# Gated linear attention and an MLP on one core: more turning by DMA, and a new order

## The chip, the cores and the metric

The kernel runs on one core of a Trainium2 chip. The metric is the device time of one execution in microseconds. The engines are named as in the profile: PE (TensorE, matrix products; PEld is its weight load), DVE (VectorE), ACT (ScalarE), POOL (GpSimd) and SP (SyncE, which here issues every DMA).

## The reference

Four batches, eight heads, 768 steps, head size 48, all float32. The attention keeps a 48x48 state for each head, decays it by a gate and adds an outer product at each step. Its outputs, the heads side by side, are the 3072 rows of 384 that go through an MLP with a silu.

```python
f = 1.0 / (1.0 + np.exp(-f_logit))
for t in range(S):
    state = f[:, :, t, :, None] * state + np.einsum('bhd,bhe->bhde', k[:, :, t], v[:, :, t])
    y[:, :, t] = np.einsum('bhd,bhde->bhe', q[:, :, t], state)
x = y.transpose(0, 2, 1, 3).reshape(B * S, H * D)      # 3072 x 384
h = x @ w_in                                           # w_in 384 x 2048
out = (h / (1.0 + np.exp(-h))) @ w_out                 # w_out 2048 x 384
```

## The kernel before

The steps are cut into chunks of 128. A *unit* is one chunk of one batch with all eight heads; there are 24. Two units make a pair P (units 2P and 2P+1), and q, k, v, f_logit are mostly loaded by pairs. In the first eight units two chunks of each batch alternate; from unit 8 on a pair is one chunk of two batches. Pairs 0 to 2 keep their rows in another interleaving (`HALF = 3`), which is why they have tasks of their own below.

The whole kernel is a list of named tasks, the string `PLAN`, in the order in which they are emitted. A word is `kind_arguments/engine/slots`: `mo_9_2/PE` is task `mo` of unit 9, part 2, on PE. Each engine works its own tasks strictly in the order of the list and waits where an operand is not ready. A slot number says which of a class's buffers a result takes (`SLOTS`); class `ps` is the eight PSUM banks, `qk` has five buffers, `qkT` three, `yb` three, `xT` four. So the list sets the order on each engine and on the DMA queue, and which buffer must be free first.

The tasks of a unit, in the order of the data:

- `f`, `q`, `k`, `v` (line 253): loads, on SP. `wi`, `wo` (291, 295) load the weights, and `wic`, `woc` (300) cast them to bf16.
- `E`, `L` (260, 262, 264): exp and log on ACT, which give the log of the gate. `cs` (356, 360), or `csh` for pairs 0 to 2 (331 to 335): its running sum, by a triangular product on PE.
- `ia`, `a`, `al` (363, 365, 368): exponentials of that sum on ACT. `qg`, `ki` (238): q and k times these, into buffer `qk`, on DVE or POOL. `vb` (231, 233, 235): v cast to bf16.
- q and k are then turned, so that the head dimension lies on the partitions. Units 0 to 9 do it by `tq` (379): eight PE transpositions into one PSUM bank, then copies out of it by `qc`, `kc` (pairs 0 to 2, line 389) or `qkc` (units 6 to 9, line 381). Units 10 to 23 do it by `qkD` (391), a DMA transposition from buffer to buffer. `dT`, `kn` (395, 397) turn k back for units 0 to 5.
- `sc2` (276): the scores of both units of a pair, 16 products. `at` (400): times the triangle, on DVE. `y` (406, 410): outputs from the old state and the scores. `d`, `sd`, `su` (432, 437, 439, 444): the new state.
- `yc`: y to bf16 in buffer `yb`. `yT` (418): y turned by three PE transpositions, and `xc` copies it to `xT`. A task `yD` (426), which turns it by DMA, is in the code, but the list does not use it.
- `mi`, `si` (319, 316): first product of a pair in eight parts of six matmuls, and the silu on ACT; `mi1`, `si1` (309, 306) the same by single units for units 0 to 5, in four parts of twelve.
- `mo` (347): second product of a unit, in four parts of four matmuls of 384 columns, all into one bank. `oc` copies it out, `so` (353) stores it.
- `idle` (287): products with zeros, which fill PE's waits at the start.

Copies share the helper's lines 231 (ACT), 233 (DVE) and 235 (POOL). ACT holds one table of functions at a time; where the list changes between exp or log and silu, a table load is emitted (line 483).

Of the kernel before, what the change touches and what calls it, by code (L numbers as in the profile page):

```python
# [30 lines left out]
f_0_1/SP/0 f_2_3/SP/1 k_0_1/SP/0 q_0_1/SP/0 q_2_3/SP/1 k_2_3/SP/1 wi_2/SP/0 v_0/SP/0 v_1/SP v_2/SP/1 wi_4/SP/1 wi_0/SP/0 wi_1/SP/1 v_3/SP E_0_1/ACT  # L31
L_0_1/ACT/0 idle_0_10_512/PE/0 csh_0/PE/0,1 E_2_3/ACT L_2_3/ACT/1 ia_1/ACT/0 a_1/ACT/0 ia_0/ACT/1 a_0/ACT/1 ki_1/DVE/0 qg_1/DVE ki_0/DVE/1 qg_0/DVE
idle_1_3_512/PE/2 csh_1/PE/2,3 idle_2_5_256/PE/1 tq_1/PE/4 idle_3_4_256/PE/1 tq_0/PE/5 a_2/ACT/2 ia_3/ACT/2 a_3/ACT/0 kc_1/DVE/0 qc_0/DVE qg_2/DVE/2
qg_3/DVE/3 qc_1/ACT kc_0/ACT ia_2/ACT/0 al_2/ACT/0 al_0/ACT/1 ki_2/DVE ki_3/POOL idle_4_4_512/PE/1 dT_0/PE/6 dT_1/PE/7 sc2_0/PE/1,3,4,5 tq_2/PE/2
idle_5_4_256/PE/0 tq_3/PE/0 kn_1/DVE/0 kc_2/ACT/1 qc_2/ACT kc_3/ACT wic_2_1/POOL vb_0/POOL/0 wic_2_0/POOL wic_2_2/POOL vb_1/POOL/1 at_0_1/DVE/0
at_1_0/DVE/1 qc_3/DVE kn_0/DVE/1 at_0_0/DVE idle_6_4_512/PE/3 d_0/PE/7 dT_2/PE/3 sc2_1/PE/4,2,6,0 y_0/PE/1 vb_2/POOL/2 yc_0/ACT/0 kn_2/ACT/1
at_1_1/DVE sd_0/DVE/0 at_2_1/DVE/2 at_2_0/DVE idle_7_3_512/PE/5 yT_0/PE/5 dT_3/PE/7 d_1/PE/1 d_2/PE/2 y_2/PE/3 xc_0/DVE/0 sd_2/DVE/1 wic_4_1/DVE
wic_4_2/DVE kn_3/ACT/0 yc_2/ACT/1 wic_4_0/ACT su_0/POOL/0 wi_3/SP/2 wo_0/SP/3 wo_1/SP/4 f_4_5/SP/2 wo_2/SP/0 wo_3/SP/1 q_4_5/SP/2 k_4_5/SP/2 f_7/SP/3
v_4/SP/2 v_5/SP f_6/SP v_6/SP/3 f_8_9/SP/0 k_6/SP/3 q_7/SP/3 q_6/SP k_7/SP y_1/PE/4 mi1_0_1/PE/5 yT_2/PE/7 xc_2/ACT/1 wic_0_0/POOL wic_0_1/ACT
yc_1/DVE/2 sd_1/DVE/0 su_2/DVE/0 wic_1_0/DVE wic_1_1/DVE at_3_1/DVE/3 at_3_0/DVE vb_3/POOL/3 mi1_0_3/PE/2 yT_1/PE/3 mi1_2_1/PE/4 mi1_2_3/PE/7  # L40
mi1_2_0/PE/1 mi1_0_0/PE/0 y_3/PE/6 si1_2_3/ACT/0 si1_0_3/ACT/1 si1_2_0/ACT si1_0_0/ACT yc_3/ACT/0 wic_3_1/ACT si1_2_1/ACT si1_0_1/ACT xc_1/DVE
wic_3_0/POOL wic_3_2/DVE mi1_1_0/PE/7 mi1_1_1/PE/2 yT_3/PE/3 mi1_1_3/PE/1 mi1_2_2/PE/0 mi1_1_2/PE/6 mi1_0_2/PE/4 d_3/PE/5 sd_3/DVE/1 woc_2_1/DVE
woc_2_0/DVE woc_2_2/DVE su_3/DVE/0 woc_3_1/DVE su_1/DVE/0 woc_3_2/DVE woc_3_0/DVE woc_0_2/POOL woc_0_1/POOL woc_1_0/POOL woc_1_2/POOL woc_1_1/POOL
si1_1_0/ACT woc_0_0/ACT si1_2_2/ACT si1_1_3/ACT si1_1_1/ACT si1_0_2/ACT xc_3/ACT si1_1_2/ACT E_4_5/ACT L_4_5/ACT/2 mo_0_0/PE/7 mo_1_0/PE/0 mo_2_0/PE/1
mi1_3_0/PE/5 mo_1_1/PE mi1_3_1/PE/2 mi1_3_3/PE/4 mo_0_1/PE csh_2/PE/3,6 al_4/ACT/2 ia_4/ACT/1 a_5/ACT/1 a_4/ACT/2 ia_5/ACT/0 vb_5/POOL/4 vb_4/POOL/5
qg_5/DVE/4 qg_4/DVE/0 ki_4/DVE si1_3_1/ACT ki_5/DVE mo_1_2/PE mo_0_2/PE mo_2_1/PE mi1_3_2/PE/3 mo_0_3/PE mo_1_3/PE tq_4/PE/6 tq_5/PE/2 oc_1/DVE/0
qc_4/DVE/2 si1_3_0/ACT si1_3_3/ACT si1_3_2/ACT kc_4/ACT kc_5/DVE qc_5/DVE E_7/ACT oc_0/DVE/1 mo_3_0/PE/5 mo_3_1/PE dT_4/PE/4 sc2_2/PE/0,3,6,2
kn_4/DVE/1 at_4_0/DVE/0 at_4_1/DVE L_7/ACT/0 E_6/ACT mo_2_2/PE d_4/PE/7 mo_3_2/PE cs_7/PE/4 y_4/PE/0 sd_4/DVE/1 at_5_0/DVE/2 at_5_1/DVE L_6/ACT
yc_4/ACT/1 ia_7/ACT/2 al_7/ACT/3 su_4/POOL/0 dT_5/PE/3 mo_3_3/PE cs_6/PE/7 yT_4/PE/6 mo_2_3/PE y_5/PE/0 ia_6/ACT/1 E_8_9/ACT a_7/ACT/0 kn_5/DVE/0
xc_4/DVE/2 oc_3/DVE/2 a_6/ACT/1 L_8_9/ACT/1 al_6/ACT/4 vb_6/POOL/0 qg_7/POOL/1 ki_6/DVE/2 yc_5/DVE/2 qg_6/DVE oc_2/DVE/3 ki_7/DVE mi1_4_0/PE/2  # L50
mi1_4_1/PE/3 d_6/PE/6 mi1_4_3/PE/5 yT_5/PE/4 mi1_4_2/PE/0 tq_6/PE/7 tq_7/PE/1 f_10_11/SP/1 q_8_9/SP/0 v_7/SP f_12_13/SP/2 q_10_11/SP/1 k_8_9/SP/0
so_1/SP k_10_11/SP/1 v_8_9/SP/0 si1_4_0/ACT/2 qkc_6/ACT/0 si1_4_2/ACT si1_4_1/ACT si1_4_3/ACT xc_5/DVE qkc_7/DVE vb_7/POOL/2 sd_6/DVE/0 su_6/DVE/0
mi1_5_1/PE/4 mi1_5_0/PE/2 mi1_5_2/PE/7 mi1_5_3/PE/1 sc2_3/PE/0,6,3,5 si1_5_2/ACT si1_5_3/ACT si1_5_0/ACT si1_5_1/ACT at_7_1/DVE/1 at_6_1/DVE/3
at_7_0/DVE at_6_0/DVE mo_4_0/PE/7 mo_4_1/PE cs_8/PE/1 cs_9/PE/2 d_5/PE/5 d_7/PE/4 mo_5_0/PE/6 y_7/PE/3 y_6/PE/0 mo_4_2/PE mo_5_1/PE yc_6/DVE/0
sd_5/DVE/1 yc_7/DVE/1 sd_7/DVE/0 E_10_11/ACT L_10_11/ACT/2 ia_8/ACT/0 cs_11/PE/0 yT_6/PE/5 mo_5_2/PE yT_7/PE/3 mo_5_3/PE mo_4_3/PE cs_10/PE/4
E_12_13/ACT ia_11/ACT/1 al_8/ACT/5 a_9/ACT/2 a_11/ACT/0 L_12_13/ACT/0 ia_9/ACT/2 a_8/ACT/1 xc_6/DVE/3 xc_7/DVE qg_9/DVE/3 ki_8/DVE/0 su_7/DVE/0
qg_8/DVE al_11/ACT/6 ia_10/ACT/0 a_10/ACT/2 oc_4/ACT/4 al_9/ACT/7 al_10/ACT/0 ki_9/DVE oc_5/DVE/0 mi_3_1/PE/5 mi_3_7/PE/3 tq_8/PE/1 mi_3_0/PE/0
mi_3_2/PE/7 tq_9/PE/2 mi_3_3/PE/4 mi_3_6/PE/6 qg_11/POOL/4 qkc_8/DVE/1 qkc_9/DVE ki_10/DVE/2 vb_9/POOL/1 qg_10/POOL vb_8/POOL/3 ki_11/POOL
si_3_2/ACT/1 si_3_1/ACT si_3_7/ACT si_3_0/ACT si_3_3/ACT so_0/SP so_5/SP v_10_11/SP/1 v_12_13/SP/2 qkD_10/SP/2 qkD_11/SP k_12_13/SP/2 so_3/SP
q_12_13/SP/2 d_9/PE/1 mi_3_4/PE/7 sc2_4/PE/2,5,3,0 mi_3_5/PE/4 sd_9/DVE/0 at_8_0/DVE/0 at_8_1/DVE at_9_1/DVE/2 at_9_0/DVE si_3_4/ACT si_3_5/ACT  # L60
si_3_6/ACT vb_11/DVE/5 cs_12/PE/1 d_8/PE/7 mo_7_0/PE/2 cs_13/PE/5 mo_7_1/PE y_8/PE/4 mo_7_2/PE y_9/PE/6 yc_8/DVE/2 yc_9/DVE/0 su_5/POOL/0 a_12/ACT/1
al_12/ACT/1 sd_8/DVE/1 a_13/ACT/0 al_13/ACT/4 vb_10/ACT/4 ia_13/ACT/2 ia_12/ACT/0 mo_7_3/PE mo_6_0/PE/0 yT_9/PE/3 mo_6_1/PE yT_8/PE/4 mo_6_2/PE
sc2_5/PE/6,5,7,1 mo_6_3/PE at_10_1/DVE/1 at_10_0/DVE at_11_1/DVE/3 at_11_0/DVE xc_8/ACT/0 xc_9/ACT oc_7/ACT/1 ki_12/POOL/1 vb_13/POOL/2 ki_13/POOL/3
qg_12/DVE oc_6/DVE/0 vb_12/DVE/0 qg_13/DVE mi_4_1/PE/4 mi_4_5/PE/3 mi_4_7/PE/2 mi_4_0/PE/5 y_10/PE/6 y_11/PE/1 mi_4_3/PE/7 mi_4_2/PE/0 si_4_5/ACT/0
yc_10/ACT/1 si_4_7/ACT yc_11/DVE/0 yT_11/PE/3 yT_10/PE/6 mi_4_6/PE/2 mi_4_4/PE/1 xc_11/ACT/1 si_4_3/ACT si_4_0/ACT si_4_2/ACT si_4_1/ACT si_4_4/ACT
si_4_6/ACT xc_10/DVE su_9/DVE/0 su_8/POOL/0 mi_5_4/PE/6 mi_5_5/PE/3 mi_5_3/PE/7 mi_5_2/PE/5 mi_5_0/PE/0 mi_5_7/PE/4 mi_5_1/PE/1 mi_5_6/PE/2
q_14_15/SP/3 f_16_17/SP/3 qkD_13/SP/0 qkD_12/SP f_18_19/SP/0 f_14_15/SP/1 q_16_17/SP/0 k_14_15/SP/3 v_14_15/SP/3 so_7/SP k_16_17/SP/0 f_20_21/SP/2
si_5_4/ACT/2 si_5_5/ACT si_5_2/ACT si_5_0/ACT si_5_7/ACT si_5_1/ACT si_5_3/ACT si_5_6/ACT sc2_6/PE/6,3,5,0 mo_9_0/PE/4 d_11/PE/1 at_12_0/DVE/0
at_12_1/DVE at_13_0/DVE/2 at_13_1/DVE sd_11/DVE/1 mo_8_0/PE/7 mo_9_1/PE y_12/PE/2 d_10/PE/6 d_13/PE/3 mo_9_2/PE d_12/PE/5 mo_8_1/PE mo_8_2/PE
y_13/PE/0 su_11/POOL/0 yc_12/DVE/2 sd_10/DVE/0 sd_13/DVE/1 yc_13/DVE/0 E_14_15/ACT L_14_15/ACT/1 E_16_17/ACT L_16_17/ACT/2 cs_17/PE/1 mo_8_3/PE  # L70
cs_15/PE/2 yT_13/PE/6 yT_12/PE/3 mo_9_3/PE cs_14/PE/0 al_15/ACT/3 a_15/ACT/2 ia_15/ACT/1 al_17/ACT/2 a_17/ACT/1 ia_14/ACT/0 al_14/ACT/5 a_14/ACT/0
ia_17/ACT/2 xc_13/DVE/2 xc_12/DVE oc_8/DVE/2 su_10/POOL/0 qg_14/DVE/0 oc_9/DVE/1 ki_14/DVE sd_12/DVE/0 ki_15/POOL/4 ki_17/POOL/2 qg_15/POOL
mi_6_5/PE/6 mi_6_1/PE/3 mi_6_6/PE/2 mi_6_4/PE/7 mi_6_3/PE/0 mi_6_0/PE/1 mi_6_2/PE/4 mi_6_7/PE/5 so_8/SP v_16_17/SP/0 qkD_15/SP/1 qkD_14/SP
q_18_19/SP/1 so_9/SP si_6_6/ACT/1 si_6_1/ACT si_6_0/ACT si_6_5/ACT si_6_2/ACT si_6_4/ACT si_6_3/ACT si_6_7/ACT mo_10_0/PE/2 cs_16/PE/3 mo_11_0/PE/1
# [86 lines left out]
def kernel(  # L161
# [117 lines left out]
    def emit(kind, a, eng):  # L279
# [95 lines left out]
        elif kind == "tq":  # L375
            t_ps = bank16("tq", u).rearrange("p (j n c) -> p j n c", j=2, c=C)
            for j in range(2):
                for p in range(NP):
                    nc.tensor.transpose(t_ps[:, j, p, :], at("qk", u)[:, j, 2 * p:2 * p + 2, :], ident)  # L379
# [135 lines left out]
```

## Time and profile before

| | |
|---|---|
| median of 3 runs | 182.08 us (182.04 to 182.3) |
| profiled execution | 181.97 us, span 180.2 us |
| PE busy | 172.5 us, 96% of the span |
| ACT, DVE, POOL busy | 131.8, 103.7, 41.5 us |
| granted PE clock | 1.0 throughout |
| DMA | 33.86 MB, mean 188 GB/s |

The span is the time from the first to the last instruction that the profile shows; the execution's own time is 1.8 us longer. Lines are those of the kernel's source; a line can be a helper's, and is then told apart by the tiles that it writes and reads (`qkT<-qk` writes `qkT` from `qk`). "Idle before" is the time that an engine stood still ahead of an instruction, with what it waited for. The chain of work that ended last goes back from the last instruction to what released it, step by step.

### The profile page before, as it was taken

The numbers are of one execution on the slowest core, as the hardware profiler recorded it, in microseconds if no ns is written. First come the engines' busy times: TensorE is split into PE (matmuls) and PEld (weight loads), VectorE is DVE, ScalarE is ACT, GpSimd is POOL, SyncE is SP. The second block draws the span as 40 slices with busy tenths as digits, with TensorE's granted clock in tenths as the row PEclk, the third lists the DMA queues.
The fourth block names the chain that finished last, engine by engine and source line by source line (L and its number), as shares of the span: only waits on it lengthen the run. The fifth ranks groups of instructions, "written<-read, shape, count | busy, mean of one in ns | idle before, by whom it ended". The sixth has DMA issues, their size and how long they took to land.

```text
span 180.2 us, 4796 instructions
## 1 busy us (share of the span) xinstructions
PE 172.5 (96%) x1969; PEld 134.8 (75%) x1971; DVE 103.7 (58%) x217; ACT 131.8 (73%) x249; POOL 41.5 (23%) x67
## 2 busy tenths in 40 slices
...
GB/s 159 322 323 303 356 392 397 230 214 213 177 176 242 101 64 188 222 234 154 234 194 222 167 195 227 261 181 92 178 262 161 160 247 4 0 87 4 0 44 131
DMA packets 110933, 33.86 MB, mean 188 GB/s; under 512 B 105280, under 2 KB 109120, under 8 KB 110912
## 3 DMA queue, kind: packets, MB, share of 16 engines
...
## 4 chain that ended last, share of the span: by engine, by line
PE 88%; DMA 4%; ACT 3%; DVE 2%; issue 0%; ACTq 0%
PE ps L347 34%; PE ps L319 25%; PE ps L309 9%; PE ps L276 4%; PE ps L410 3%; PE ps L418 2%; PE ps L379 2%; PE ps L432 2%; PE ps L406 2%; DMA f<-in_f_logit_dram 2%; DMA qkT<-qk 2%; ACT qkT L231 2%; PE ps L356 2%; DVE qk L238 1%; PE ps L287 1%; PE ps L395 1%
## 5 line engine op out<-in xcount | busy, mean ns | idle before, releaser
L347 PE MATMUL ps<-w_out,hT 128*128 128x384 bf16 x384 | 70.5, 326 | 0.0
L319 PE MATMUL ps<-xT,w_in 128*128 128x256 bf16 x432 | 50.4, 273 | 0.0
L347 PEld LDWEIGHTS <-hT 128*128 128x128 bf16 x384 | 34.8, 98 | 19.4
L319 PEld LDWEIGHTS <-w_in 128*128 128x128 bf16 x432 | 45.1, 110 | 1.8
L316 ACT ACTIVATE hT<-ps 128x512 bf16<-128x512 f32 x72 | 37.3, 612 | 7.6 <-PE ps L319 7.4
L400 DVE TENSOR_TENSOR at<-ps,triu 128x512 bf16<-128x512 f32 x36 | 22.4, 684 | 18.3 <-PE ps L276 16.9
L233 DVE COPY ob<-ps 128x384 f32<-128x384 f32 x16 | 8.8, 550 | 19.5 <-PE ps L347 19.5
L483 ACT ACT_TABLE_LOAD x15 | 19.2, 1283 | 0.3
L309 PE MATMUL ps<-xT,w_in 128*128 128x128 bf16 x288 | 18.1, 219 | 0.0
L309 PEld LDWEIGHTS <-w_in 128*128 128x128 bf16 x288 | 16.8, 110 | 0.4
L238 POOL TENSOR_TENSOR st<-sd,al 48x192 bf16<-48x192 f32 x18 | 9.8, 547 | 29.3 <-DVE sd L437 11.5
L238 POOL TENSOR_TENSOR qk<-k,ia 128x384 bf16<-128x384 f32 x9 | 9.3, 1036 | 26.2 <-DMA k<-in_k_dram 9.6
L437 DVE TENSOR_TENSOR sd<-ps,st 128x384 f32<-128x384 f32 x16 | 8.8, 550 | 10.7 <-ACT hT L316 5.2
L238 POOL TENSOR_TENSOR qk<-q,av 128x384 bf16<-128x384 f32 x7 | 8.0, 1155 | 29.5 <-ACT av L365 29.5
L238 DVE TENSOR_TENSOR qk<-k,ia 128x384 bf16<-128x384 f32 x15 | 12.3, 836 | 4.0 <-ACT ia L363 4.0
L306 ACT ACTIVATE hT<-ps 128x512 bf16<-128x512 f32 x24 | 13.0, 628 | 0.1
L238 DVE TENSOR_TENSOR qk<-q,av 128x384 bf16<-128x384 f32 x17 | 10.5, 629 | 4.2 <-ACT av L365 3.8
L231 ACT COPY xT<-ps 128x384 bf16<-128x384 bf16 x10 | 5.0, 515 | 10.6 <-PE ps L418 10.6
L363 ACT ACTIVATE ia<-ps 128x384 f32<-128x384 f32 x24 | 11.7, 496 | 1.2 <-PE ps L356 0.7
L260 ACT ACTIVATE f<-f 128x768 f32<-128x768 f32 (+1 forms) x13 | 10.3, 792 | 2.2 <-DMA f<-in_f_logit_dram 2.1
L365 ACT ACTIVATE av<-ps 128x384 f32<-128x384 f32 x24 | 11.4, 501 | 0.0
L287 PE MATMUL ps<-zero 128*128 128x512 bf16 (+1 forms) x35 | 9.8, 411 | 1.3 <-DVE zero L461 1.2
...
## 6 DMA issues: line engine op xcount, KB each, us to landing
...
```

Of the source, the lines that this page charges most:

```text
L238: (nc.vector if eng == "DVE" else nc.gpsimd).tensor_mul(*a)
L260: nc.scalar.activation(e, e, AF.Exp, scale=-1.0)
L287: nc.tensor.matmul(at("idle", u)[:, 0:w], zero[:, 0:128], zero[:, 0:w], start=True, stop=True)
L306: return nc.scalar.activation(at("hT", u // 2)[:, 4 * m:4 * m + 4, i * C:(i + 1) * C], h, AF.Silu)
L309: nc.tensor.matmul(h[:, n, :], w_in_tile(4 * m + n, kk), at("xT", u // 2)[:, kk, i * C:(i + 1) * C], start=(kk == 0), stop=(kk == KT - 1))
L316: return nc.scalar.activation(at("hT", P)[:, 2 * j:2 * j + 2, :], h, AF.Silu)
L319: nc.tensor.matmul(h[:, i, :], w_in_tile(2 * j + i, kk), at("xT", P)[:, kk, :], start=(kk == 0), stop=(kk == KT - 1))
L347: nc.tensor.matmul(o, at("hT", P)[:, n, i * C:(i + 1) * C], w_out_sb[n // 4][:, n % 4, :], start=(n == 0), stop=(n == NT - 1))
L363: nc.scalar.activation(at("ia", u).rearrange("p h d -> p (h d)"), at("cs", u)[:, 0:HD], AF.Exp)
L365: nc.scalar.activation(at("av", u).rearrange("p h d -> p (h d)"), at("cs", u)[:, 0:HD], AF.Exp, scale=-1.0)
L400: nc.vector.tensor_mul(at("at", u)[:, r], at(f"s{r}", u).rearrange("p (n c) -> p n c", c=C), (triup if two else triu)[:, None, :].to_broad ...
L483: nc.scalar.preload_act_table_set(turn[n])
```

## The change

1. `qkD` is also used for units 6 to 9, in the place of `tq` and `qkc`: 18 in place of 14.
2. `yD` is used for units 12 to 21, in the place of `yT` and `xc`: ten.
3. In units 0 to 5 (`APART`) the turned k goes to a second PSUM bank (`tqk`), so that `qc` and `kc` read different banks.
4. The second product of units 22 and 23 goes by `moh`, `och`, `soh`: each column half of 192 in a bank of its own, copied and stored by itself.
5. The list is in a new order throughout, with new slots, and some tasks have another engine. `ki` and `qg` on POOL go from 16 to 24, table loads from 15 to 19, products with zeros from 37 to 29. `SLOTS` is as before.

```diff
+APART = {0, 1, 2, 3, 4, 5}
...
-"tq": lambda: [(("tq", u), "ps")],
+"tq": lambda: [((x, u), "ps") for x in (("tq", "tqk") if u in APART else ("tq",))],
+"moh": lambda: [(("oB" if a[1] else "o", u), "ps")], "och": lambda: [(("ob", u), "ob")],
...
+        elif kind == "moh":
+            w = d_model // 2
+            o = at("oB" if a[1] else "o", u)[:, 0:w]
+            for n in range(4 * a[2], 4 * a[2] + 4):
+                nc.tensor.matmul(o, at("hT", P)[:, n, i * C:(i + 1) * C], w_out_sb[n // 4][:, n % 4, a[1] * w:(a[1] + 1) * w],
+                                 start=(n == 0), stop=(n == NT - 1))
+        elif kind == "och":
+            w = d_model // 2
+            copy(eng, at("ob", u)[:, a[1] * w:(a[1] + 1) * w], at("oB" if a[1] else "o", u)[:, 0:w])
+        elif kind == "soh":
+            r0, w = b * S + c * C, d_model // 2
+            nc.sync.dma_start(out=out[r0:r0 + C, a[1] * w:(a[1] + 1) * w], in_=at("ob", u)[:, a[1] * w:(a[1] + 1) * w])
...
-            t_ps = bank16("tq", u).rearrange("p (j n c) -> p j n c", j=2, c=C)
             for j in range(2):
                 for p in range(NP):
+                    t_ps = bank16("tqk" if j and u in APART else "tq", u).rearrange("p (j n c) -> p j n c", j=2, c=C)
                     nc.tensor.transpose(t_ps[:, j, p, :], at("qk", u)[:, j, 2 * p:2 * p + 2, :], ident)
...
-            copy(eng, dst, bank16("tq", u)[:, 512 * j:512 * (j + 1)].rearrange("p (w c) -> p w c", c=64))
+            copy(eng, dst, bank16("tqk" if j and u in APART else "tq", u)[:, 512 * j:512 * (j + 1)].rearrange("p (w c) -> p w c", c=64))
```

The new list, in the places that the prediction speaks of. The start:

```
f_0_1/SP/0 f_2_3/SP/1 q_0_1/SP/0 k_0_1/SP/0 E_0_1/ACT f_4_5/SP/2 L_0_1/ACT/0 E_2_3/ACT idle_0_11_512/PE/0 csh_0/PE/0,1 v_0/SP/0 a_0/ACT/0 v_1/SP
ia_0/ACT/0 qg_0/DVE/0 a_1/ACT/1 ki_0/DVE q_2_3/SP/1 ia_1/ACT/1 qg_1/DVE/1 L_2_3/ACT/1 idle_1_8_512/PE/2 tq_0/PE/2,3 k_2_3/SP/1 ki_1/DVE E_4_5/ACT
kc_0/DVE/0 idle_2_4_256/PE/1 tq_1/PE/4,5 csh_1/PE/6,7 qc_0/DVE wi_3/SP/0 kc_1/ACT qc_1/DVE vb_1/POOL/0 al_0/ACT/0 vb_0/DVE/1 a_2/ACT/2
sc2_0/PE/1,3,2,4 wi_2/SP/1 L_4_5/ACT/2 dT_0/PE/5 qg_2/POOL/2 at_0_1/DVE/0 a_3/ACT/0 at_1_0/DVE/1 kn_0/ACT/0 idle_3_2_512/PE/0 csh_2/PE/0,3 qg_3/POOL/3
at_1_1/DVE al_2/ACT/1 ia_3/ACT/2 wi_1/SP/0 d_0/PE/2 dT_1/PE/5 at_0_0/DVE a_4/ACT/1 ki_3/POOL al_4/ACT/2 ia_2/ACT/0 sd_0/DVE/0 idle_4_4_256/PE/4
y_0/PE/7 ia_5/ACT/1 ki_2/DVE tq_3/PE/4,1 a_5/ACT/2 kn_1/DVE/1 su_0/POOL/0 ia_4/ACT/2 tq_2/PE/6,2 v_2/SP/1 qc_3/DVE/1 yc_0/ACT/0 d_1/PE/3 kc_2/DVE
kc_3/ACT yT_0/PE/5 wic_3_0/POOL y_1/PE/0 wi_0/SP/1 qc_2/DVE xc_0/ACT/0 wic_3_2/POOL dT_2/PE/4 yc_1/DVE/1 wic_3_1/ACT sc2_1/PE/7,2,1,6 wic_2_1/POOL
v_3/SP kn_2/DVE/0 wic_2_0/ACT yT_1/PE/5 dT_3/PE/0 wic_2_2/DVE mi1_0_2/PE/4
```

PE's tasks from the outputs of units 18 to 21 to the first product of their pairs:

```
y_19 mo_17_2 y_18 d_16 cs_20 cs_21 mo_16_1 mo_15_3 d_19 mo_16_2 mo_16_3 d_18 mo_17_3 mi_9_4
y_20 cs_23 mo_19_0 y_21 cs_22 mo_18_1 mo_18_2 mo_18_3 mo_19_1 mo_19_2 mo_19_3 mi_10_2
```

PE's end, from the last scores on:

```
sc2_11 mo_21_0 mo_20_1 mo_21_1 mo_21_2 y_22 y_23 mo_21_3 yT_22 mo_20_2 yT_23 mo_20_3 mi_11 (8 parts) moh (16 parts)
```

SP's tasks from unit 6 to pair 5, and at the end:

```
q_6 k_7 q_7 v_6 v_7 qkD_6 qkD_7 k_8_9 q_8_9 so_3 f_10_11 v_8_9 qkD_9 v_10_11 qkD_8 f_12_13 f_14_15 k_10_11 q_10_11 k_12_13 f_16_17 v_12_13 qkD_11 qkD_10
q_22_23 so_14 k_22_23 yD_20 yD_21 so_16 so_12 qkD_22 qkD_23 so_8 so_13 so_18 so_19 so_15 so_17 so_21 so_20 soh_23_0 soh_22_1 soh_22_0 soh_23_1
```

More of the change, by code (lines that the diff above doesn't have):

```diff
@@ L30 @@
 PLAN = """
[L31 to L74, printed above, removed]
```

91 lines of the change are left out of this document (64 added, 27 removed).

## The prediction

> **What bounds the kernel now.** I read the page's busy times first, then engine use by stretch, then the waits, then the chain that ended last.
>
> ```profile
> span 180.2 us, 4796 instructions
> PE 172.5 (96%) x1969; PEld 134.8 (75%) x1971; DVE 103.7 (58%) x217; ACT 131.8 (73%) x249; POOL 41.5 (23%) x67
> ```
> ```profile
> 20.07:46.00 25.93, 25.93 (x358) 21.27 (x356) 17.87 (x41) 23.97 (x45) 6.99 (x12) 1.00 1.04 293
> 46.00:100.00 54.00, 53.15 (x675) 44.29 (x673) 36.85 (x68) 46.33 (x89) 15.76 (x21) 1.00 0.96 187
> 100.00:148.00 48.00, 47.52 (x499) 36.94 (x498) 30.29 (x60) 35.84 (x69) 11.58 (x15) 1.00 0.96 194
> 148.00:176.90 28.90, 28.80 (x266) 21.91 (x263) 4.89 (x9) 12.63 (x27) 0.00 (x0) 1.00 0.08 29
> ```
> ```profile
> PE ps L379 <- DVE qk L238: 0.8, 1, 0.8
> PE ps L276 <- DMA qkT<-qk: 0.5, 1, 0.5
> DVE qkT L233 <- ACT qkT L231: 0.8, 1, 0.8
> ```
>
> In the stretches (the columns are length, then busy time and count of PE, PEld, DVE, ACT and POOL, clock, DMA share, GB/s) PE is idle for 0.00 + 0.85 + 0.48 + 0.10 = 1.4 us between 20.07 and 176.9, nearly all of it in the two PE waits listed above. So from 20 us on, each instruction taken off PE moves the end, unless something else is late. The second thing to see is the DMA share: 1.04, 0.96, 0.96, then 0.08. The DMA engines are as full as PE until 148 us and empty afterwards. A change that moves work from PE to DMA spends from a full account; only the empty 29 us at the end can pay.
>
> ```profile
> 19.88 0.20 PE ps L410 x8
> 20.07 0.68 PE ps L309 x12
> ...
> 24.57 0.17 PE ps L406 x4
> ...
> 39.41 0.89 PE ps L379 x16
> ...
> 59.12 0.65 PE ps L347 x4
> ...
> 77.14 2.62 PE ps L319 x24
> ...
> 81.82 0.35 PE ps L418 x6
> ...
> 167.06 9.76 PE ps L347 x60
> ...
> 176.84 0.48 ACT ob L231
> ```
>
> These pieces of the chain (start, duration, what) are the prices on PE: a transposition (L379, L418) 0.056 us, a part of the second product `mo` 0.65, a `mi` 2.62/4 = 0.66, a `y` 0.20 or, with old state, 0.37.
>
> **Part by part. Turning off PE.** `tq` of units 6 to 9 goes: 4 x 8 x 0.056 = 1.8 us. `yT` of units 12 to 21 goes: 10 x 3 x 0.056 = 1.7 us. Both sit where PE has no idle time, so 3.5 us leave the path. The four `qkc` and ten `xc` copies go too, from ACT and DVE, which the stretches show with room (from 46 to 100 us ACT is busy 46.33 and DVE 36.85 of 54): no gain of their own.
>
> **The order at the start.** Before the first `mi1` (20.07) PE mostly waits, between warm-up products, for the copies of the turned q and k. The new start can be followed with these rows.
>
> ```profile
> 7.37 0.47 ACT L363 ACTIVATE ia<-ps 128x384 f32<-128x384 f32 x1
> ...
> 7.74 0.48 ACT L365 ACTIVATE av<-ps 128x384 f32<-128x384 f32 x1
> ...
> 7.87 0.56 DVE L238 TENSOR_TENSOR qk<-k,ia 128x384 bf16<-128x384 f32 x1 [3.85 <-ACT ia L363]
> ...
> 8.35 0.55 DVE L238 TENSOR_TENSOR qk<-q,av 128x384 bf16<-128x384 f32 x1
> ...
> 9.91 1.31 DVE L233 COPY qkT<-ps 128x512 bf16<-128x512 bf16 x2
> ...
> 10.68 1.30 ACT L231 COPY qkT<-ps 128x512 bf16<-128x512 bf16 x2 [0.53 <-DVE qkT L233]
> ...
> 12.22 0.26 ACT L368 ACTIVATE al<-ps 128x8 f32<-128x8 f32 x2
> ...
> 17.94 0.48 ACT L231 CAST yb<-ps 128x384 bf16<-128x384 f32 x1 [2.31 <-PE ps L410]
> ...
> 18.31 0.59 ACT L231 COPY kn<-ps 128x512 bf16<-128x512 bf16 x1
> ...
> 20.12 0.63 ACT L231 CAST w_in<-ws 128x512 bf16<-128x512 f32 x1
> ```
> ```profile
> 5.01 0.85 ACT lf L262
> ...
> 7.36 0.67 PE ps L287 x3
> 8.03 0.16 PE ps L331
> ...
> 8.68 0.18 PE ps L335 x8
> ...
> 12.66 0.55 PE ps L276 x16
> ```
>
> `csh_0` still ends at about 7.36. DVE forms the four q, k products 0.47 apart, to 9.83. Then `kc_0`, `qc_0`, `qc_1` follow on DVE at 0.6 each, to 11.6, while ACT, after `L_2_3` and `E_4_5` (0.85 each), copies `kc_1` from another bank, to 11.3. So `sc2_0` starts at 11.65 against 12.66 (L276). (The warm-up products, 37 before and 29 now, 0.22 each, only fill such waits: the eight ahead of `tq_0` end at 9.1, 0.2 after `ki_0`, on nobody's path.) That ACT and DVE take turns on one bank is the third wait above. (The Trainium skill, "PSUM — Partial Sum Buffer", section "PSUM bank collisions raise a hardware error", tells to guard by bank, not by address, reads against reads too; by it a bank each is what allows the two copies side by side, and the trace agrees, with the 0.8 us wait.) After 11.3 ACT has seventeen operations ahead of the first `mi1`: `al` x3 at 0.2, eight exponentials at 0.4, `L_4_5` 0.85, `kn_0` 0.6, `yc_0` 0.4, `kc_3` 0.7, `xc_0` 0.5, `wic_3_1` 0.6: 7.5 us, so `mi1_0_2` starts at about 18.85, 1.2 us earlier, with 0.7 us more done (`csh_2`, four products of 0.16 and eight of 0.02, is already behind; a `d` less a `yT`, and a `y`, are not). A lead of 1.9 us.
>
> I keep only 0.4 of it. The DMA share from 20 to 46 us is 1.04 already, and the loads ahead of `sc2_3` are the same bytes plus `v_7`. A transposition stands in SP's queue behind these loads, so PE's lead runs into q and k of units 6 to 13. Ends of this term: a gain of 1.9, if nothing is late, and a loss of 1.2, if one transposition is late by half of what the slowest landing below is over the median (2.4 us).
>
> **The transpositions on SP and the DMA engines.**
>
> ```profile
> L391 SPq DMA_TRANSPOSE qkT<-qk x14: 1231/1268/2601, 67.7 to 144.4; - x14
> ...
> DMA to landing us min/median/max: 3.1/3.3/5.7
> ```
>
> SP gets 14 more issues of 1.27 us at most, 18 us; what queues behind each on SP is loads for later pairs. At 190 GB/s (the rate of the two full stretches) a q, k transposition of 256 KB costs the engines 1.38 us and one of y, 96 KB, 0.52: 4 x 1.38 + 10 x 0.52 = 10.7 us. The old order ended the full stretch at 148. Four fewer whole outputs of 192 KB (1.03 each) go ahead of the last transposition now: 148 + 10.7 - 4.1 = 154.6 us is when q and k of unit 23 would be in. PE wants them for `sc2_11`, which the new order puts 7 `mo` + two `y` + two `yT` + 8 `mi` + 16 half parts + itself = 4.6 + 0.7 + 0.3 + 5.3 + 5.2 + 0.7 = 16.8 us before the end of PE. With PE's end at 172.8 that is 156.0. So DMA just keeps up, with 1.4 us to spare; I add no wait.
>
> For y, the time on PE from the last `y` of a pair to its first `mi` is, from the new order at the prices above, 5.4 us (units 12, 13), 6.1, 5.9, 4.1 and 4.1 (20, 21). From it goes `yc`, about 0.5. With the median landing of 3.3 all five fit, the last two by 0.3. With the worst, 5.7, they are late by 0.8, 0.1, 0.3, 2.1, 2.1: 5.4 us. A transfer of y is smaller than any in that row, so I take the median end: 0.
>
> (The Trainium skill, "DMA: Bandwidth & Descriptors", section "Anatomy of one DMA", gives a fixed 2.0 us plus bytes over 436 GB/s, for another issue path; as an estimate from that page a transposition of y lands in 2.2 us and one of q, k in 2.6. The trace has 3.3 for q, k, so the measurement decides; by the page's figure the five windows would all hold with over 1 us to spare.)
>
> **Last products in column halves.** 32 products of 384 columns become 64 of 192. The chain has 9.76/60 = 0.163 for 384 columns, 0.056 for 128, 0.043 for 96 (L406): linear, so 0.081, no change in sum. Ends: 0 and +2 (if a 192-wide product took the mean of the 128- and 384-wide). The last copy halves: ACT's 0.48 becomes about 0.33, and the last transfer is half as large: -0.15. The ends here are -0.5 and +0.1.
>
> **ACT.**
>
> ```profile
> L483 ACT ACT_TABLE_LOAD x15 | 19.2, 1283 | 0.3
> ```
>
> The new order switches tables 19 times: 4 more loads, 5.1 us on ACT. From 46 to 148 us ACT has 7.7 + 12.2 us free, so nothing; with that cover gone, each switch holds up the PSUM banks that `mi` waits for, 5.1 us in all. POOL gets eight more of the q, k products and is busy 41.5 of 180, so nothing there either.
>
> **Sum.** -1.8 - 1.7 - 0.4 - 0.15 = -4.05 on a span of 180.2: 176.1. The profiled execution took 181.97 in all, so 177.9; the median of the runs, 182.08, stands 0.1 above it. I say 178.0.
>
> **Rivals.** (1) Transpositions land late. They share SP's queue and the engines with loads, and the slowest of the 14 took 5.7 where the median is 3.3. If half of the 5.4 us of the y windows comes true, 177.9 + 2.7 = 180.6. For it: y of units 18 to 21 has 0.3 us of slack. Against: before, 14 transpositions cost PE one wait of 0.5. (2) DMA becomes the bound, slower. Stretches with transpositions move fewer bytes:
>
> ```profile
> 101.00:107.00 6.00, 6.00 (x46) 4.05 (x44) 0.23 (x1) 5.87 (x11) 3.46 (x6) 1.00 1.04 140
> 122.80:129.00 6.20, 6.20 (x59) 5.56 (x56) 1.02 (x3) 5.92 (x13) 0.00 (x0) 1.00 0.83 128
> ```
>
> That is 56 GB/s under 190 for 12.2 us, or 3.6 us lost on four transpositions. At 0.9 each, 14 new ones lose 12.6 us, `sc2_11` comes at 167.2 instead of 156.0, and the time is 189. It decides from a loss of 1.4 + 4.1 = 5.5 us on: 0.4 each. Against: the second stretch begins with SP waiting for q and k, which is no lost rate; I price the case at 184. (3) The lead of the start is kept whole: 177.9 - 1.5 = 176.4. (4) ACT's four switches show up, by half: 180.5. (5) The change does nothing, since DMA returns just what PE saves: 182.
>
> **How the numbers follow.** Forecast 0.60 (176.9 to 179.3); late landings 0.14; lead kept 0.10; ACT 0.04; nothing 0.04; DMA bound 0.08. The times of this kernel agree within 0.26 us, so 0.2% (0.36 us) is about what can be told from no change. Faster: 0.60 + 0.14 + 0.10 + 0.04 = 0.88, less 0.01 where late landings eat all: 0.87; same 0.04; slower 0.09. The range 176.2 to 180.8 takes in the lead kept and half-late landings, and leaves out about 0.16.
>
> **What would show it.** PE's busy time at 167.5 to 169 with idle time after 20 us still under 3 us; the first `mi1` at 18.9 and `sc2_0` at 11.7; L379 x48 and L418 x42; waits of PE on `qkT` and `xT` under 1 us together; DMA share near 1 until some 150 us. Wrong if PE waits on `xT<-yb` or `qkT<-qk` by more than 2 us, if the DMA share stays at 1 while PE idles, or if ACT's silu falls behind the `mi` after a table load.

## The result, and the profile after

The changed kernel takes 179.06 us (median; 178.73 to 179.66) against 182.18 for the kernel before on the same chip: ratio 0.9833, 95% interval 0.9803 to 0.9862. That is 3.1 us less, where 4.1 were forecast; a second set of runs (`control`, below) gives 0.9841. In this and all that follows disturbed executions are left out. The profiled execution is the slowest of the first set: 179.66 in all, span 177.8. A profile shows one execution, and where that one lies far from the median of its version the text below says so.

The page of the changed kernel, busy times and the main DMA queue (before, 81.8% of the span of 16 engines there):

```profile
span 177.8 us, 4767 instructions
## 1 busy us (share of the span) xinstructions
PE 168.5 (95%) x1933; PEld 132.6 (75%) x1933; DVE 90.3 (51%) x190; ACT 139.5 (79%) x258; POOL 50.9 (29%) x77
...
q1 hardware_dynamic: 119584, 35.60, 89.2%
```

Engine use by stretch, in the columns that the prediction names:

```profile
20.07:46.00 25.93, 24.98 (x347) 20.40 (x347) 14.24 (x30) 23.74 (x46) 11.67 (x19) 1.00 0.96 268
46.00:100.00 54.00, 52.45 (x635) 41.38 (x634) 31.57 (x61) 45.96 (x86) 16.42 (x20) 1.00 1.08 201
100.00:148.00 48.00, 47.78 (x505) 37.88 (x504) 25.08 (x48) 40.02 (x70) 11.49 (x17) 1.00 0.94 191
148.00:174.00 26.00, 26.00 (x256) 21.67 (x255) 6.55 (x12) 14.56 (x28) 3.33 (x3) 1.00 0.38 109
```

PE has 4.0 us less to do, but now stands idle for 0.95 + 1.55 + 0.22 = 2.7 us behind 20.07, where it was 1.4. All the growth lies ahead of 100 us, where the DMA share is 0.96 and 1.08. PE's waits (total, times, longest) say for what:

```profile
PE ps L279 <- DMA qkT<-qk: 1.3, 3, 0.7
...
PE ps L394 <- POOL qk L241: 1.2, 2, 0.9
PE ps L312 <- ACT xT L234: 1.1, 1, 1.1
...
PE ps L322 <- DMA xT<-yb: 0.2, 1, 0.2
```

L279 is `sc2`, L312 `mi1`, L322 `mi`, L394 `tq`. The 1.2 of `tq` lies in the start; the 1.1 is `mi1_1_2` at 20.7 us, waiting for the copy `xc_1`; the other two rows are transpositions that landed late. In the chain that ended last these are the places where it leaves PE for a transposition, some of what leads up to them, and its end:

```profile
47.83 4.87 DMA qkT<-qk
...
60.99 4.32 DMA qkT<-qk
...
89.77 2.29 POOL qk L241 x2
92.06 1.82 SPq L406
...
93.98 4.75 DMA qkT<-qk
...
137.26 2.31 DMA xT<-yb
...
169.47 5.29 PE ps L356 x64
174.83 0.32 ACT ob L234
```

So `qkD_7`, `qkD_8`, `qkD_15` and `yD_18` each held PE. By engine, the chain was made up like this before (first row) and is now (second row):

```profile
PE 88%; DMA 4%; ACT 3%; DVE 2%; issue 0%; ACTq 0%
```
```profile
PE 56%; SPq 19%; DMA 17%; ACT 3%; POOL 2%; issue 1%; DVE 0%; ACTq 0%; POOLq 0%
```

Until `qkD_7` lands at 52.7 us this chain holds no work of PE at all: but for one copy on POOL it runs through SP's issues and the landings of loads. What PE gains before then is not on this path. In the second profile of the changed kernel (`control`) PE's share is 50%. PE's end went from 176.84 to 174.83, and what follows it from 180.2 - 176.84 = 3.4 us to 177.8 - 174.83 = 3.0.

### The profile page after: what moved, and what is told of

It is laid out like the page before. It is cut to its first block, busy times and chain, and to the rows that moved or that the text cites. A ratio compares the mean times of both kernels' runs of the same rounds, so it can differ in the third digit from the quotient of the medians.

```text
span 177.8 us, 4767 instructions
## 1 busy us (share of the span) xinstructions
PE 168.5 (95%) x1933; PEld 132.6 (75%) x1933; DVE 90.3 (51%) x190; ACT 139.5 (79%) x258; POOL 50.9 (29%) x77
## 2 busy tenths in 40 slices
DMA packets 119605, 35.89 MB, mean 202 GB/s; under 512 B 113696, under 2 KB 117792, under 8 KB 119584
## 4 chain that ended last, share of the span: by engine, by line
PE 56%; SPq 19%; DMA 17%; ACT 3%; POOL 2%; issue 1%; DVE 0%; ACTq 0%; POOLq 0%
PE ps L322 22%; PE ps L350 21%; SPq L256 13%; DMA qkT<-qk 8%; DMA ws<-in_moe_w_out_dram 5%; SPq L294 4%; PE ps L356 3%; PE ps L279 2%; DMA v<-in_v_dram 2%; PE ps L425 2%; SPq L298 2%; PE ps L312 2%; PE ps L421 1%; DMA xT<-yb 1%; POOL qk L241 1%
## 5 line engine op out<-in xcount | busy, mean ns | idle before, releaser
L350 PE MATMUL ps<-w_out,hT 128*128 128x384 bf16 x352 | 66.4, 326 | 0.0
L322 PE MATMUL ps<-xT,w_in 128*128 128x256 bf16 x432 | 50.8, 273 | 0.2 <-DMA xT<-yb 0.2
L322 PEld LDWEIGHTS <-w_in 128*128 128x128 bf16 x432 | 45.1, 110 | 3.7 <-issue 1.1
L319 ACT ACTIVATE hT<-ps 128x512 bf16<-128x512 f32 x72 | 38.3, 603 | 10.8 <-PE ps L322 10.4
L350 PEld LDWEIGHTS <-hT 128*128 128x128 bf16 x352 | 31.9, 97 | 16.8
L498 ACT ACT_TABLE_LOAD x19 | 24.4, 1283 | 0.3
L241 POOL TENSOR_TENSOR qk<-k,ia 128x384 bf16<-128x384 f32 x13 | 14.2, 1099 | 20.3 <-ACT ia L378 10.4
L312 PE MATMUL ps<-xT,w_in 128*128 128x128 bf16 x288 | 18.9, 219 | 1.2 <-ACT xT L234 1.1
L241 POOL TENSOR_TENSOR qk<-q,av 128x384 bf16<-128x384 f32 x11 | 11.8, 1078 | 25.4 <-ACT av L380 17.1
L312 PEld LDWEIGHTS <-w_in 128*128 128x128 bf16 x288 | 17.3, 109 | 2.1 <-issue 1.5
L241 POOL TENSOR_TENSOR st<-sd,al 48x192 bf16<-48x192 f32 x22 | 11.6, 526 | 15.2 <-DVE sd L454 7.5
L238 POOL CAST vb<-v 128x384 bf16<-128x384 f32 x10 | 5.6, 568 | 33.3 <-DMA v<-in_v_dram 33.2
L236 DVE COPY ob<-ps 128x384 f32<-128x384 f32 (+1 forms) x15 | 8.1, 538 | 13.4 <-PE ps L356 8.4
L241 DVE TENSOR_TENSOR qk<-q,av 128x384 bf16<-128x384 f32 x13 | 8.5, 660 | 10.0 <-ACT av L380 7.9
L234 ACT CAST yb<-ps 128x384 bf16<-128x384 f32 x13 | 6.2, 481 | 7.1 <-PE ps L425 6.9
L279 PE MATMUL ps<-qkT 48*128 48x128 bf16 x192 | 8.0, 218 | 1.4 <-DMA qkT<-qk 1.3
```

The source lines that it names most:

```text
L241: (nc.vector if eng == "DVE" else nc.gpsimd).tensor_mul(*a)
L279: nc.tensor.matmul(at(f"s{r}", u).rearrange("p (n c) -> p n c", c=C)[:, p, :], turned(u, 1, p, rows), turned(u, 0, p, rows), start=True, s ...
L312: nc.tensor.matmul(h[:, n, :], w_in_tile(4 * m + n, kk), at("xT", u // 2)[:, kk, i * C:(i + 1) * C], start=(kk == 0), stop=(kk == KT - 1))
L319: return nc.scalar.activation(at("hT", P)[:, 2 * j:2 * j + 2, :], h, AF.Silu)
L322: nc.tensor.matmul(h[:, i, :], w_in_tile(2 * j + i, kk), at("xT", P)[:, kk, :], start=(kk == 0), stop=(kk == KT - 1))
L350: nc.tensor.matmul(o, at("hT", P)[:, n, i * C:(i + 1) * C], w_out_sb[n // 4][:, n % 4, :], start=(n == 0), stop=(n == NT - 1))
```

## The experiments

Two theories. **Theory 1**: until about 98 us PE runs at the pace at which rows arrive, so what PE saves there is given back at the next late landing. **Theory 2**: PE's work and each wait add up, wherever they lie. Ratios are to the kernel before, run in the same group. For differences between versions I take the changed kernel at 179.2 us, the median of its ten runs. These spread by 178.1 to 180.7, so differences under about 0.7 us are not resolved by time alone. The changed kernel itself ran beside e_start, e_qk_pe and e_y_pe only (as `control`), not beside the others.

| run | median, us | ratio | 95% interval |
|---|---|---|---|
| control (the changed kernel) | 179.3 | 0.9841 | 0.980 to 0.988 |
| e_start | 179.4 | 0.9844 | 0.981 to 0.988 |
| e_late_22 | 179.0 | 0.9815 | 0.980 to 0.983 |
| e_one_bank | 179.8 | 0.9858 | 0.981 to 0.991 |
| e_late_113 | 180.5 | 0.9905 | 0.987 to 0.994 |
| e_qk_pe | 180.0 | 0.9878 | 0.984 to 0.992 |
| e_y_pe | 182.4 | 1.0005 | 0.998 to 1.003 |
| e_old_y | 198.4 | 1.0853 | 1.080 to 1.091 |
| e_both | 181.7 | 0.9974 | 0.995 to 1.000 |
| e_early | 181.1 | 0.9929 | 0.990 to 0.996 |
| e_less | 178.4 | 0.9786 | 0.977 to 0.980 |
| e_whole | 180.1 | 0.9892 | 0.985 to 0.993 |

### What the lead is worth: control, e_start, e_late_22, e_one_bank, e_late_113

> The changed kernel again, as the zero of this group. Both theories: 179.1 us, within 0.5, profiled span 177.8; PE's summed waiting between its first and last product about 15 us again.

Measured: 179.3, span 178.0.

e_start, on ACT's list:

```
- ... wic_2_0/ACT yT_1/PE/5 dT_3/PE/0 wic_2_2/DVE mi1_0_2/PE/4 xc_1/ACT ...
+ ... yT_1/PE/5 dT_3/PE/0 wic_2_2/DVE mi1_0_2/PE/4 xc_1/ACT wic_2_0/ACT ...
```

> One move on ACT: the conversion wic_2_0, which waits for wi_2, goes behind xc_1, for which mi1_1_2 waits. Theory 1 (until about 98 us PE is held to the rows that arrive and to SP's queue, so PE time saved before that is given back at the next product that waits for turned q, k): the 1.1 us wait at mi1_1_2 goes, sc2_3 still waits for qkD_7 landing at about 52.7 us, and the time is within 0.3 us of the control. Theory 2 (the sum of PE's work and each of its waits counts): 1.0 us below the control.

Measured: 179.4. The row `PE ps L312 <- ACT xT L234` is gone from its waits, and the time is the control's, as Theory 1 has it. Theory 2's 1.0 lies at the edge of what the two intervals leave open, and the wait varies from run to run (1.1 and 0.8 us in the two profiles of the changed kernel, 0.2 in e_late_113's, none in e_late_22's), so this run alone does not settle it.

e_late_22 and e_late_113, on PE's list:

```
+ idle_30_7_512/PE/4 mi1_0_1/PE/4      (e_late_22)
+ idle_30_7_512/PE/3 mi_7_7/PE/3       (e_late_113)
```

> Seven empty products of 512 columns (7 x 0.215 = 1.5 us of PE, on zeros) are put before mi1_0_1, at about 22 us; nothing else is changed. It takes most of the start's lead of 1.9 us away again. Theory 1 (until about 98 us PE waits for what the loads bring, so a lead is given back): the waits behind 40 us (0.3 to 0.7 us each) shrink by as much, and the time is 0 to 0.5 us above the changed kernel's 179.3. Theory 2 (each us of PE counts wherever it lies): 1.5 us above.

Measured: 179.0, 0.2 below the changed kernel, where Theory 2 wanted 1.5 above. The stretches of this run show in part how 1.5 us of empty work can be free:

```profile
20.07:46.00 25.93, 25.74 (x350) 20.80 (x351) 14.79 (x29) 22.89 (x45) 11.12 (x18) 1.00 1.03 280
46.00:100.00 54.00, 53.16 (x645) 42.22 (x643) 32.46 (x60) 46.58 (x89) 17.00 (x21) 1.00 1.01 197
```

PE is idle 0.19 + 0.84 = 1.0 us in these two, where the changed kernel has 2.5 in its first profile and 0.76 + 0.96 = 1.7 in `control`'s. Not all of that is the empty products' doing: the wait at `mi1_1_2` lies ahead of them, at about 20.7 us, and is absent in this execution. Behind 46 us the waits shrank by 0.1 to 0.7 us, so the profile shows only a part of the 1.5 taking the place of waits. That all of it is free is what the times say, 179.0 against 179.2: a lead at 22 us is worth less than the runs can tell.

> The same seven empty products before mi_7_7, at about 114 us. The waits behind it are those of mi_9_4 for yD_18 (0.4 and 1.0 us in two profiled runs) and of mi_10_2 (0 and 0.6). Theory 1: 0.3 to 1.0 us above the changed kernel's 179.3, since these shrink. Theory 2: 1.5 us above.

Measured: 180.5, 1.3 above. By 113 us most of a PE microsecond counts; this is nearer to Theory 2's 1.5 than to the middle of Theory 1's range, though by the ratios, 0.9905 - 0.9841, it is 1.2, and the intervals do not exclude the upper end of that range. The plainest comparison is with e_late_22, which ran beside it: the same seven products cost 180.5 - 179.0 = 1.5 us more at 113 us than at 22.

e_one_bank, the bank part of the change undone:

```
- APART = {0, 1, 2, 3, 4, 5}
+ APART = {99}
```

> Turned q and k of units 0 to 5 share one bank again, all else as in the changed kernel. The first products sc2_0 then wait for the copy of both, 0.5 to 1.0 us later than 10.9 us. As the lead was worth nothing in the run with empty products at 22 us: within 0.4 us of the changed kernel's 179.3. If the start counts: 0.5 to 1.0 us above.

Measured: 179.8, so +0.5, inside the spread. `sc2_0` starts at 11.75 instead of 10.8 (10.9 in `control`), as expected. The interval holds both 0 and 0.5; the run does not separate the theories, but it agrees with the one above.

### The transpositions undone one by one: e_qk_pe, e_y_pe

```
- qkD_6/SP ... qkD_7/SP ... qkD_9/SP ... qkD_8/SP
+ tq_6/PE qkc_6/DVE ... tq_7/PE qkc_7/DVE ... tq_9/PE qkc_9/DVE ... tq_8/PE qkc_8/DVE      (e_qk_pe)
- yD_12/SP to yD_21/SP
+ yT_12/PE xc_12/ACT ... to yT_21/PE xc_21/ACT      (e_y_pe)
```

> q, k of units 6 to 9 turned on PE again (32 products and four copies), all else as in the changed kernel. PE has 1.8 us more work, all of it before 65 us, and the waits for qkD_7 (0.65 us) and qkD_8 (0.23 us) go. Theory 1: +0.3 us to +0.5 us against the control, as loads further down still set sc2_7. Theory 2: +0.9 to +1.8 us.

Measured: 180.0, so +0.8 for 1.8 us of PE work. The estimates of the two theories meet near there, so the time alone decides little; the stretch from 46 to 100 us does. PE is busy in all of it, at a DMA share of 0.94 instead of 1.08:

```profile
46.00:100.00 54.00, 54.00 (x665) 43.15 (x663) 33.57 (x64) 46.35 (x87) 17.13 (x21) 1.00 0.94 181
```

So turning q, k of units 6 to 9 by DMA takes 1.8 us from PE and puts about 1 us of waiting in its place (in this stretch PE is idle 1.55 us in the changed kernel's first profile, 0.96 in `control`'s). The profiled execution of e_qk_pe, 178.95, is 1.0 below its median.

> y of units 12 to 21 turned on PE again (30 products and ten copies out of PSUM), all else as in the changed kernel. PE has 1.7 us more work behind 98 us. As the prediction sized it: 1.7 us above the control, less the 0.4 us that mi_9_4 waits for yD_18 now, so +1.3 (180.4). Rival, that the ten transposition issues on SP (1.2 us each) hold up the loads of q, k: less than +0.7, since sc2_7 no longer waits 0.4 us and what follows moves up.

Measured: 182.4, so +3.2, a miss: 1.9 more than the sum and far above the rival. The waits of PE:

```profile
PE ps L279 <- DMA qkT<-qk: 1.6, 4, 0.6
...
PE ps L433 <- DVE at L415: 0.3, 1, 0.3
```

Late landings did not shrink. PE is idle behind 20.07 us for 0.28 + 1.45 + 1.26 = 3.0 us, against 2.7 in the changed kernel's profile, so the waits give back nothing of the 1.7 us that PE now works more; `yT` waits once, for 0.3 us (L433), and no row shows `mi` waiting on PE for `xc`. That makes 2.0 us; the two profiled executions lie 2.3 apart, the medians 3.2, and what makes up the rest is not shown. The places of `yT` and `xc` in this version are mine, and a better order might take some of it back.

### The operation without the new order: e_old_y

The kernel before and its own order, in it `yT`, `xc` of units 12 to 21 replaced:

```
- yT_13/PE/6 yT_12/PE/3 ... xc_13/DVE/2 xc_12/DVE
+ yD_13/SP/2 yD_12/SP                                  (so for each pair)
```

> The kernel before with its own order, and in it y of units 12 to 21 turned by DMA (30 products and ten copies go; q_20_21, k_22_23, v_22_23 go behind yD_14 on SP). It does the operation without the order made for it. By the sum: 1.7 us of PE less, but the first products of blocks 6 and 10 follow their copies yc by about 2 us, less than the 3.3 us in which a transposition lands there, so 1 to 2 us of waits each: 181.5 to 184. If the order matters little: 180.4.

Measured: 198.4, 16 us slower than before, and 14 outside my estimate. PE's largest wait, what the trace has on the line that issues the y transpositions, and a stretch:

```profile
PE ps L318 <- DMA xT<-yb: 10.9, 4, 5.1
```
```profile
L425 SPq DMA_TRANSPOSE xT<-yb x10: 1185/1206/2417, 96.9 to 172.5; - x10
...
DMA to landing us min/median/max: 2.3/2.4/4.5
```
```profile
100.00:148.00 48.00, 40.94 (x387) 30.91 (x388) 18.57 (x37) 27.78 (x53) 7.48 (x11) 0.93 0.83 168
```

A landing takes 2.4 us in the median, no more than in the changed kernel (2.7). What I had left out is the time that the issue stands in SP's queue, as the longest of these waits, 5.1 us, shows: `yc_12` is done at 92.6 us, `yD_12` goes out at 99.4, behind `f_20_21` and `yD_13`, lands at 101.8, and `mi_6_5` starts at 101.9. The new order is what makes the operation pay: it puts 4.1 to 6.1 us of other products between a pair's `y` and its `mi` (the prediction's windows), and `yD_12` there goes out 1.2 us after `yc_12` (97.9, then 99.1). The places of `yD` on SP in e_old_y are mine (`yD_13` ahead of `yD_12`, though `yc_12` comes first), so how much a better place in the old order would save is not shown.

Not all of the 16 us is waiting. The waits for `xT` and `qkT` are 10.9 + 2.5 us, where they were 0.5. Most of the rest is PE itself: it is busy 176.4 us, against 172.5, although 1.7 us of its work is gone. The granted clock is 0.974 in the mean of this execution and 0.93 in the stretch above, where the kernel before and the changed one have 1.0. That the clock falls because PE waits is not isolated by any run here.

### Which landings, or all of them: e_both, e_early, e_less

Theory 1 leaves open whether a few late landings hold PE, which an order could mend, or the load of the DMA engines as a whole.

e_both, on SP's list (with e_start's move and `vb_7` behind `xc_5`):

```
- v_6 v_7 qkD_6 qkD_7 ... v_10_11 qkD_8 ... qkD_13 v_16_17 qkD_14 ... yD_13 yD_12 q_16_17 ... so_4 so_11 yD_19 yD_18
+ v_6 qkD_6 qkD_7 v_7 ... qkD_8 v_10_11 ... qkD_13 qkD_14 ... yD_13 yD_12 v_16_17 q_16_17 ... yD_19 yD_18 so_4 so_11
```

> Orders alone: on SP the loads v_7, v_10_11, v_16_17 and the stores so_4, so_11 go behind the transpositions that PE waits for next (qkD_7, qkD_8, yD_12, yD_18); on ACT wic_2_0 goes behind xc_1; on DVE vb_7 goes behind xc_5. Theory 1 (transpositions that land late hold PE): the waits at sc2_3, sc2_4, sc2_7 and mi_9_4, 1.7 us together in the first profiled run, go, and the start's lead is kept: 1.5 to 2.5 us below the changed kernel's 179.3. Theory 2 (the DMA engines as a whole are the limit until about 150 us, whatever the order): within 0.5 us, with the waits at other places.

Measured: 181.7, 2.5 slower than the changed kernel, which neither theory expected. The waits at `sc2_3`, `sc2_4` and `mi_9_4` did go: `qkT<-qk` holds PE for 0.2 us in all, and `xT<-yb` for nothing that the list shows. In their place:

```profile
PE ps L350 <- DVE ob L236: 1.7, 1, 1.7
```

This is `mo_12_0` at 108.5, waiting for the output copy `oc_11`. The chain into it:

```profile
106.96 0.36 DVE qk L241
...
107.43 0.55 DVE qk L241
107.98 0.48 DVE ob L236
...
108.50 0.81 PE ps L350 x4
```

`oc_11` stands on DVE behind `ki_17` and `ki_16` (L241), the products that need `k_16_17`. The chain puts their start down to ACT's silu (hT), of which they read nothing; the load had landed at 106.86, 0.1 us before, and I take it for the releaser. From 100 to 109 us that load took 6.7 us from issue to landing, against 4.9 in the changed kernel. The row of e_both:

```profile
k<-in_k_dram SPq DMA_DIRECT2D x1, 384.0 KB, 6.7
```

In the changed kernel `mo_12_0` starts at 108.6 as well: what was won ahead of it was given back by there. So this wait explains why nothing was won, not why time was lost. The two profiled executions stay level until about 137 us; then e_both's falls 1.0 us behind, and its chain says how:

```profile
138.72 2.19 DMA out_dram<-ob
...
140.93 0.48 ACT ob L234
...
145.33 1.47 PE ps L322 x12
```

The store `so_4`, moved behind `yD_18`, now lands at 140.9. `oc_16` takes the buffer that `so_4` empties and waits for it on ACT; the table load and the silu of pair 9 stand behind `oc_16`, and PE goes on with `mi` at 145.33, where the changed kernel does at 144.35. This is a loss made by my own move. It accounts for 1.0 us in this execution, which at 180.6 is 1.1 below e_both's median; the rest of the 2.5 is not explained.

e_early, the moves up to 65 us alone, and `so_6`, whose landing frees the buffer of `oc_11`, ahead of `v_14_15`:

```
- ... v_14_15 yD_13 yD_12 q_16_17 k_16_17 so_6 yD_14 yD_15 ...
+ ... so_6 v_14_15 yD_13 yD_12 q_16_17 k_16_17 yD_14 yD_15 ...
```

> The moves of the last combined run up to 65 us alone (on SP v_7 behind qkD_7 and v_10_11 behind qkD_8, on DVE vb_7 behind xc_5, on ACT wic_2_0 behind xc_1), and the store so_6 nine places earlier on SP, ahead of v_14_15, since oc_11 and so mo_12_0 waited for its landing at 107.3 us. If single landings hold PE: mo_12_0 starts at about 107 instead of 108.6 and the time is 1.0 to 1.6 us below the changed kernel's 179.3. If the DMA engines as a whole pin PE until about 125 us: the wait shows again at sc2_8 (qkD_16) or later, and the time is within 0.4 us.

Measured: 181.1, 1.9 above the changed kernel; again worse than either expectation. Its profiled execution took 182.6, well above its median, so I read no row from it. Neither of my two attempts to mend single landings by order worked, and the order in place is better than both.

e_less:

```
- v_6/SP/3 v_7/SP  so_0 so_1 so_2 so_3 so_5 so_6 so_7
- copy(eng, at("vb", u), at("v", P)[:, i])
+ copy(eng, at("vb", u), at("v", 2 if P == 3 else P)[:, i])
```

> Leaves out the loads v_6, v_7 (units 6 and 7 read the v of units 4 and 5) and the stores of units 0 to 3 and 5 to 7: 1.4 MB less for the DMA engines between 38 and 105 us, PE's work the same. If the DMA engines' load sets the waits there: sc2_3, sc2_4, sc2_7 no longer wait, 1.0 to 1.8 us below the changed kernel's 179.3. If the waits come of each transposition's own time from its issue: within 0.4 us.

Measured: 178.4; by the ratios 0.9841 - 0.9786 = 0.0055, or 1.0 us below `control`, the low edge of the first expectation. (What is left out is 35.89 - 34.12 = 1.77 MB by the two pages, not the 1.4 I wrote.) The stretches say it more plainly than the time, though the profiled execution, 176.8, is 1.6 below its median:

```profile
20.07:46.00 25.93, 25.74 (x358) 21.03 (x358) 14.25 (x31) 23.78 (x45) 11.34 (x18) 1.00 0.99 269
46.00:100.00 54.00, 53.76 (x656) 42.54 (x654) 33.22 (x64) 46.14 (x88) 17.27 (x21) 1.00 0.95 181
100.00:148.00 48.00, 47.91 (x494) 37.87 (x490) 24.41 (x47) 41.74 (x72) 12.41 (x18) 1.00 0.90 181
```

PE is idle 0.19 + 0.24 + 0.09 = 0.5 us instead of 2.7, with the order untouched. Some 0.8 of this difference is not the change's doing: the wait at `mi1_1_2`, at 20.7 us, is absent in this execution, ahead of anything that was left out. Behind 46 us PE is idle for 0.3 us, where both profiles of the changed kernel have 1.8 (1.55 + 0.22 and 0.96 + 0.87), and no transposition is left in the chain that ended last. This speaks for the amount that SP and the DMA engines have to bring until about 100 us, and not for one landing, as what holds PE there. It is not quite separated from the order: `v_6` and `v_7` stood right ahead of `qkD_6` and `qkD_7`. But e_both, which moved `v_7` and `v_10_11`, lost the waits at `sc2_3` and `sc2_4` as well and gained no time. Bytes and issues were not told apart: nine issues fewer stand on SP, too, seven of them stores.

### The halves undone: e_whole

```
- moh_23_1_0/PE/6 ... och_23_0/DVE/3 ... soh_23_1/SP
+ mo_23_0/PE/4 mo_22_0/PE/1 ... oc_22/DVE/3 mo_23_3/PE so_22/SP oc_23/ACT/2 so_23/SP
```

> The last two units' products, copies and stores whole instead of in column halves. As the prediction sized it: 0.15 us above the changed kernel's 179.3, less than the runs can tell; in the profile the span from PE's last product to the end grows from 3.0 us by 0.1 to 0.3 us, and PE's work is the same within 0.2 us.

Measured: 180.1, +0.9, with the spread as above. The end of its chain:

```profile
168.93 5.38 PE ps L348 x32
174.32 0.48 ACT ob L232
```

The whole products take 5.38 us where the halves take 5.29, so the sum on PE is the same. From PE's end to the end of the span it is 177.8 - 174.32 = 3.5 us against 3.0: the halves bring 0.5 us at the tail, 0.16 of it in the last copy (0.48 to 0.32), the rest in the store.

## Why the prediction was right, and where it was off

**Turning off PE, -3.5**: right as work of PE. L394 (`tq`) runs x48, L433 (`yT`) x42, as forecast. PE's busy time fell by 4.0, of which the warm-up products are part. As time it is right only in sum, and that is luck: undone one by one, the two parts, priced 1.8 and 1.7, cost 0.8 (e_qk_pe) and 3.2 (e_y_pe).

**Start**: `mi1_0_2` came at 18.78 (18.85 forecast). `sc2_0` came at 10.8, 0.85 earlier than forecast: the copies of the turned q and k began on DVE at 9.34, not at 9.83, and took 0.45 us each, not 0.6. "I keep only 0.4 of it" was wrong. PE's end moved by 176.84 - 174.83 = 2.0; with 3.5 us less work, the start and all waits together cost 1.5 instead of bringing 0.4. This is the term that failed, by 1.9 us, with two parts. In the profiled execution 1.1 us of the lead went at once, at `mi1_1_2`: I had followed ACT's list only to the first `mi1`, and `wic_2_0`, ahead of `xc_1`, waits for `wi_2`. The rest went as the prediction says, into waits for turned q and k, of units 6 to 9 and of 14 and 15, but all of it; by e_late_22 no part of a lead at 22 us that the runs could tell arrives at the end.

**Transpositions on SP and DMA, "I add no wait"**: half right. The end of the chain of DMA holds: in the last stretch, from 148 us, PE is busy 26.00 of 26.00. But `qkD_7`, `qkD_8` and `qkD_15` held PE for 1.3 us, against 0.5 before. The loss was priced as -1.2 to +1.9 around the start; it came out just beyond its lower end. e_less and e_qk_pe show the cause: the account was full ahead of 100 us, and the 148 + 10.7 - 4.1 sum looked only at its end. The 1.27 us "at most" for an issue on SP is the median of the row it was read from, whose longest is 2.60; in the changed kernel the longest are 2.45 and 3.08. And POOL's extra products were not quite "nothing": ahead of `qkD_15` the chain stands on POOL with `ki_14`, which was DVE's before, and `qg_15`, and at the start `tq` waits 1.2 us for POOL.

**The y windows, median landing, 0**: nearly right in this trace, with 0.2 us of waiting; 1.4 in `control`'s, of 5.4 in the worst case. They landed in 2.7 us in the median (3.1 in `control`), faster than the 3.3 taken over from q, k. (The Trainium skill, "DMA: Bandwidth & Descriptors", section "Anatomy of one DMA", from which the prediction worked out 2.2 for y and 2.6 for q, k: for y the least landing, 2.3, agrees; for q, k the trace has 3.1 at least and 3.6 in the median here, so there it does not.)

```profile
DMA to landing us min/median/max: 2.3/2.7/4.5
```
```profile
DMA to landing us min/median/max: 3.1/3.6/4.9
```

**Halves, -0.15**: right in kind, too small; 0.4 between the two profiles and 0.5 in e_whole. I had priced the store's half at almost nothing; by the list of DMA issues a store of 96 KB lands in 1.6 us, one of 192 KB in 2.3:

```profile
out_dram<-ob SPq DMA_DIRECT2D x22, 192.0 KB, 2.3
...
out_dram<-ob SPq DMA_DIRECT2D x4, 96.0 KB, 1.6
```

**ACT, 0**: right as far as the waits show: ACT has 19 table loads, 24.4 us, and no row of PE's waits in the changed kernel names ACT's silu. In `control`'s chain two table loads do stand, at 37.79 and 80.21 us, and no version has fewer of them, so their price was not isolated.

**Sum.** In the profiled execution: -3.5 + 1.5 - 0.4 = -2.4 (180.2 to 177.8); by the medians -3.1. Of the rivals, the lead kept whole is refuted, the kernel did not get slower with DMA as its bound, and the late landings came in a smaller form than the 2.7 us priced, in q and k more than in y in the first profile (1.3 and 0.2 us), the other way in `control`'s (1.0 and 1.4). Of its signs, PE's busy time (168.5), its idle time (2.7) and the counts came as said. PE's waits on `qkT` and `xT`, 1.5 us together, are over the 1 us stated, and one sign of being wrong did show: from 46 to 100 us the DMA share is 1.08 while PE idles.

The causes of e_both's and e_early's loss are only in part shown: in e_both the wait at `mo_12_0` takes back what was won ahead of it, and the late store `so_4` costs 1.0 us behind it, both in one execution. e_early leaves that store where it was and is slower all the same; why stays open.
